# Reordering the first batch of a fused attention and mixer kernel, and the start of its second

## The chip, the cores and the metric

One core of a Trainium2 chip. The metric is the device time of one execution in microseconds (us). The kernel before takes 277.95 us (median of four executions, 277.54 to 278.02). Engines carry their short names in profile lines: PE (TensorE's matmuls), PEld (its weight loads), DVE (VectorE), ACT (ScalarE), POOL (GpSimd), SP (SyncE, which issues transfers).

## The reference

Eight batches of linear attention, then an MLP mixer on its output.

```python
# attention; phi(x) = x + 1 for x > 0, else exp(x)
q_p, k_p = phi(q), phi(k)                          # q, k, v: (8, 8, 576, 64) fp32
kv = einsum('bhsd,bhse->bhde', k_p, v);  z = sum(k_p, axis=2)
x = einsum('bhsd,bhde->bhse', q_p, kv) / (einsum('bhsd,bhd->bhs', q_p, z)[..., None] + 1e-6)
# mixer; x as (8, 576, 512)
h  = maximum(x^T @ w_tok1, 0) @ w_tok2             # over the 576 tokens
u  = x + h^T
out = u + maximum(u @ w_ch1, 0) @ w_ch2            # 512 -> 1536 -> 512
```

## The kernel before

The program gives each engine its instructions in a fixed order, and the traces show them run in it. So a place in that order is a decision: an instruction that waits for data holds up all behind it on its engine. mm1 and mm2 are the two products over tokens, mm3 and mm4 the two over channels. In the names of steps, qtr and qt transpose phi(q), kv forms the product of phi(k) and v, nd forms x's numerator and denominator (num and den divide them), vcast rounds v, warm runs matmuls that compute nothing, and utr transposes u into uT. mm3 and mm4 of one batch are the dense work; a list called `fill` places the next batch's small steps behind numbered pieces of it. While batch 0 is prepared, there is nothing dense to run.

phi, as three instructions per half of k or q (exp on ScalarE, the rest on VectorE):

```python
def phi_exp(nm, n, j0, nj):   nc.scalar.activation(out=e, in_=f, func=AF.Exp)          # f: raw k or q
def phi_add(nm, n, j0, nj):   nc.vector.tensor_scalar(out=y, in0=f, scalar1=1.0, op0=ALU.add)
def phi_end(nm, n, j0, nj):   # e = min(e, 1), then out = max(e, y), both on VectorE
```

mm3 writes a tile in one of four PSUM banks, and a relu empties it (cut):

```python
def mm3(n, mc, kjs=range(NDM)):
    ps = part_of[mc]                              # from the pool ps_big, four banks
    for kj in kjs:
        nc.tensor.matmul(out=ps, lhsT=wc1[:, kj, 128 * mc:128 * mc + 128], rhs=uT[b][:, :, kj], ...)
    if kjs[-1] == NDM - 1:
        nc.scalar.activation(out=cr[b][:, mc, :], in_=ps, func=AF.Relu)
```

mm4 of batch 0 takes its four output tiles from the same four banks, so its first piece needs the relus of mm3's last four tiles. Batch 0's order, and where batch 1's steps stand among its twelve tiles of mm3 (slots 0 to 11) and twelve pieces of mm4 (slots 12 to 23), both cut:

```python
e_first("k", 1); k_first(1, 0); k_first(1, 1)
nd_first(0); warm(24)
e_first("q", 1); q_first(1, 0); vcast(0, 1)
den_first(0); q_first(1, 1); qtr_first(1, [act, act]); kv_first(1, act)
# ... num, mm1 ...
mm2_first(0, [0, 1], False); mm1_first(1, [R])
mm2_first(0, [2, 3], True); mm2_first(1, [0, 1], True)   # True: x added by an identity matmul, ScalarE copies u
mm2_first(1, [2, 3], False)
utr_first(0); mm3 (tiles 0 to 2, half of their products); utr_first(1)

landed[...] = load(nm, 1, c, c_in[0] if nm == "k" and c == 0 else None)     # q right behind k
c2_in += [after(load_wc2(i), landed["q1", 1] if i == 1 else None) for i in range(1, NB)]

fill = [(1, mm2_first_tail)]
fill += [(5, phi k half 0), (8, phi k half 1), (11, phi q half 0), (12, phi q half 1)]
at0 = {"qt0": 13, "qt1": 14, "kv": 15, "nd00": 16, ..., "mm1": 22, "mm2a": 23, ...}
```

`load(..., gate)` issues a transfer only once another has landed: batch 1's k waits for the first quarter of the weight wc1 (issued at 12.86 us in the profile before, 6.9 us to landing; k is issued at 19.73), and wc2's second quarter waits for batch 1's q (issued at 34.95, after 17.83 us of waiting for q).

## Time and profile before

| kernel before | |
|---|---|
| median, range | 277.95 us, 277.54 to 278.02 |
| span of the profiled execution | 275.8 us |
| TensorE busy | 261.5 us, 95% |
| from where TensorE has no gaps | 62 us |

### The profile page before, as it was taken

What the parts mean: (1) busy time and instruction counts of PE and PEld (TensorE: products, weight loads), DVE (VectorE), ACT (ScalarE), POOL (GpSimd) and SP (SyncE); (2) the same over time, 40 slices, a digit from 0 to 9 for tenths busy, and PEclk for the clock granted to TensorE, in tenths of its full rate; (3) what the DMA queues carried; (4) which work ended last, traced back from release to release, by engine and by line L of the source; (5) the groups of instructions that cost most, each with busy time, mean ns of one, the idle gap of its engine ahead of it and who ended that gap; (6) DMA issues with size and microseconds to landing.
All of it is one profiled execution on the core that took longest, in us unless ns stands there. A gap on an engine that the chain in (4) does not pass through costs nothing.

```text
span 275.8 us, 4751 instructions
## 1 busy us (share of the span) xinstructions
PE 261.5 (95%) x1924; PEld 141.0 (51%) x1924; DVE 153.3 (56%) x300; ACT 141.3 (51%) x211; POOL 31.2 (11%) x52
## 2 busy tenths in 40 slices
PE   8678888989999999999999999999999999999993
PEld 8665335544664465445564464445464554444641
DVE  3762274749576957793768347875676271520121
ACT  5634697149974376814666066806673155016400
POOL 4640030004001030011000210011001300000000
PEclk9999999999999999999999999999999999999998
DMA  7999999996002899689918970384045500740043
GB/s 267 293 167 260 358 171 273 400 404 171 2 0 64 205 351 407 272 186 253 402 33 190 351 305 0 71 155 110 0 76 129 133 21 0 134 110 5 2 103 88
DMA packets 45190, 47.73 MB, mean 173 GB/s; under 512 B 25520, under 2 KB 30000, under 8 KB 45168
## 3 DMA queue, kind: packets, MB, share of 16 engines
q1 hardware_dynamic: 37632, 35.53, 41.4%
q0 software_dynamic: 6896, 10.85, 18.2%
q10 hardware_dynamic: 640, 1.05, 1.0%
q8 instruction: 15, 0.25, 0.3%
q14 instruction: 7, 0.06, 0.1%
HBM read 35.85 MB, written 9.44 MB: 164 GB/s over the span
## 4 chain that ended last, share of the span: by engine, by line
PE 87%; ACT 5%; DVE 3%; DMA 2%; issue 1%; SPq 0%; ACTq 0%
PE h_ps L464 32%; PE c_ps L441 28%; PE a_ps L236 5%; PE h_ps L248 5%; PE c_ps L452 4%; PE nd_ps L198 3%; PE kv_ps L157 3%; ACT e L115 2%; DMA q_raw<-in_q_dram 2%; DVE qp L130 1%; PE bank L382 1%; PE tp L168 1%; PE bank L367 1%; PE bank L318 1%; DVE e L129 1%
## 5 line engine op out<-in xcount | busy, mean ns | idle before, releaser
L445 ACT ACTIVATE cr<-c_ps 128x512 bf16<-128x512 f32 x96 | 55.9, 600 | 74.3 <-PE c_ps L441 74.2
L441 PE MATMUL c_ps<-uT,wc 128*128 128x512 bf16 x384 | 91.3, 379 | 1.9 <-ACT uT L407 1.1
L464 PE MATMUL h_ps<-wc,cr 128*128 128x512 bf16 x384 | 88.3, 379 | 0.0
L464 PEld LDWEIGHTS <-cr 128*128 128x128 bf16 x384 | 37.0, 98 | 42.4 <-issue 0.3
L441 PEld LDWEIGHTS <-wc 128*128 128x128 bf16 x384 | 35.8, 98 | 38.6 <-issue 2.7
L481 DVE TENSOR_TENSOR o_sb<-h_ps,u 128x512 f32<-128x512 f32 x32 | 21.7, 688 | 24.1 <-PE h_ps L464 24.0
L486 POOL DMA_DIRECT2D out_dram<-o_sb x24 | 14.9, 625 | 160.7 <-DVE o_sb L481 160.4
L210 DVE TENSOR_TENSOR x<-nd_ps,den 128x512 bf16<-128x512 f32 (+1 forms) x42 | 25.3, 602 | 1.5
L129 DVE TENSOR_SCALAR e<-e 128x1152 bf16<-128x1152 bf16 x30 | 14.5, 485 | 16.3 <-ACT e L115 16.1
L260 DVE TENSOR_TENSOR u<-h_ps,x 128x1024 bf16<-128x1024 f32 x13 | 15.5, 1219 | 13.0 <-PE h_ps L248 13.0
L115 ACT ACTIVATE e<-k_raw 128x1152 bf16<-128x1152 f32 x16 | 18.8, 1172 | 2.6 <-DMA k_raw<-in_k_dram 2.6
L207 DVE TENSOR_SCALAR den<-nd_ps 128x8 f32<-128x8 f32 (+1 forms) x42 | 6.8, 163 | 23.6 <-PE nd_ps L198 23.0
L248 PE MATMUL h_ps<-ar,w2p 128*128 128x512 bf16 x70 | 18.9, 379 | 0.2
L115 ACT ACTIVATE e<-q_raw 128x1152 bf16<-128x1152 f32 x16 | 18.5, 1168 | 0.5 <-DMA q_raw<-in_q_dram 0.5
L141 ACT CAST vs<-v_raw 128x1152 bf16<-128x1152 f32 x14 | 16.3, 1162 | 1.2 <-DMA v_raw<-in_v_dram 1.2
L198 PEld LDWEIGHTS <-qT 128*128 128x128 bf16 x140 | 11.5, 98 | 9.6 <-issue 0.2
L239 ACT ACTIVATE ar<-a_ps 128x512 bf16<-128x512 f32 x14 | 7.6, 595 | 16.9 <-PE a_ps L236 16.9
L198 PE MATMUL nd_ps<-kvbd,qT 128*128 128x130 bf16 x140 | 15.1, 223 | 0.0
L236 PE MATMUL a_ps<-x,w 128*128 128x512 bf16 x56 | 14.4, 379 | 0.0
L491 DVE TENSOR_TENSOR o_sb<-h_ps,ut 128x512 f32<-128x512 f32 x4 | 2.8, 690 | 18.7 <-PE h_ps L464 18.7
L130 DVE TENSOR_TENSOR qp<-e,y 128x1152 bf16<-128x1152 bf16 x16 | 12.1, 759 | 0.6
L121 DVE TENSOR_SCALAR y<-q_raw 128x1152 bf16<-128x1152 f32 x16 | 12.1, 754 | 0.2
(91 smaller groups left out, 222.1 us busy)
## 6 DMA issues: line engine op xcount, KB each, us to landing
k_raw<-in_k_dram SPq DMA_DIRECT2D x16, 576.0 KB, 6.3
q_raw<-in_q_dram SPq DMA_DIRECT2D x16, 576.0 KB, 11.1
v_raw<-in_v_dram SPq DMA_DIRECT2D x16, 576.0 KB, 9.1
out_dram<-o_sb POOLq DMA_DIRECT2D x24, 256.0 KB, 3.9
wc<-in_moe_w_ch_dram POOLq DMA_DIRECT2D x8, 384.0 KB, 8.7
out_dram<-o_sb SPq DMA_DIRECT2D x10, 128.0 KB, 2.3
out_dram<-o_sb ACTq DMA_DIRECT2D x8, 128.0 KB, 2.6
out_dram<-o_sb POOLq DMA_DIRECT2D x6, 128.0 KB, 6.0
```

The costliest lines, as they stand in the source:

```text
L115: nc.scalar.activation(out=e, in_=f, func=AF.Exp)
L129: nc.vector.tensor_scalar(out=e, in0=e, scalar1=1.0, scalar2=None, op0=ALU.min)
L141: copy(out=vs[:, js, :, 0:D], in_=raw["v", n % 2][:, js].rearrange("p j (t d) -> p j t d", t=T))
L198: nc.tensor.matmul(out=o[:, a], lhsT=qT[b][:, t0:t0 + 128], rhs=kvbd[b][:, c, a], start=True, stop=True)
L210: nc.vector.tensor_tensor(out=x[b][:, rs[0]:rs[0] + m, HG * D * g:HG * D * (g + 1)].rearrange("p r (h d) -> p r h d", h=HG), in0=v_[:, :, ...
L236: nc.tensor.matmul(out=ps[:, mt], lhsT=w1t[:, b, ms] if r == R else w1[:, r, ms], rhs=x[b][:, r, :], start=(r == 0), stop=(r == R))
L248: nc.tensor.matmul(out=ps[:, i], lhsT=w2v(kt, r, b), rhs=ar[b][:, kt, :], start=(kt == 0), stop=(kt == NT - 1 and not add))
L260: nc.vector.tensor_tensor(out=u[b][:, rs[0]:rs[0] + m], in0=ps[:, 0:m], in1=x[b][:, rs[0]:rs[0] + m], op=ALU.add)
L441: nc.tensor.matmul(out=ps, lhsT=wc1[:, kj, 128 * mc:128 * mc + 128], rhs=uT[b][:, :, kj], start=(kj == 0), stop=(kj == NDM - 1))
L445: nc.scalar.activation(out=cr[b][:, mc, :], in_=ps, func=AF.Relu)
L464: nc.tensor.matmul(out=ps, lhsT=crt[:, kc, :] if t == 8 else cr[b][:, kc, 128 * r:128 * r + 128], rhs=wc2[:, kc, :], start=(kc == 0), stop ...
L481: nc.vector.tensor_tensor(out=o, in0=ps, in1=u[b][:, r, :], op=ALU.add)
```

## The change

The intent, in three parts. **First batch:** VectorE's work on k's second half moves into a gap; den waits behind q; mm1 of the first half is done in one piece; u's sums all go to VectorE and the four identity matmuls go; the transpositions of u are split. **Batch 1 sooner:** phi of k and q stands from slot 2 instead of slot 5, which puts exp ahead of relus of mm3; three relus go to VectorE; q's load gets a gate; the attention steps from kv on move up one slot (in batch 1's own mixer, which the cut below leaves out, nd moves down one). **End of batch 1's mixer:** mm2 by column halves, and mm3 begun on half of u.

```diff
 e_first("k", 1)
 k_first(1, 0)
+kv_first(0, dve)
 k_first(1, 1)
-nd_first(0)
-warm(24)
 e_first("q", 1)
 q_first(1, 0)
 vcast(0, 1)
-den_first(0)
+nd_first(0)
+warm(14)
 q_first(1, 1)
+den_first(0)
 ...
-mm2_first(0, [0, 1], False)
 mm1_first(1, [R])
-mm2_first(0, [2, 3], True)
-mm2_first(1, [0, 1], True)
-mm2_first(1, [2, 3], False)
-utr_first(0)
-for mc in range(3):
+mm2_first(0, [0, 1])
+mm2_first(0, [2, 3])
+mm2_first(1, [0, 1])
+utr_first([0, 1], act)
+mm2_first(1, [2, 3])
+mm3(0, 0, range(0, 2))
+utr_first([2], act)
+utr_first([3], dve)
+for mc in range(1, 3):
     mm3(0, mc, range(0, 2))
-utr_first(1)
 ...
-load(nm, 1, c, c_in[0] if nm == "k" and c == 0 else None)
+load(nm, 1, c, {"k": c_in[0], "q": c_in[3]}.get(nm) if c == 0 else None)
 ...
+mm3(0, mc, dve=mc in (3, 5, 8))              # relu on VectorE for these
-at0 = {"qt0": 13, "qt1": 14, "kv": 15, "nd00": 16, ...
+at0 = {"qt0": 13, "qt1": 14, "kv": 14, "nd00": 15, ...
-fill = [(1, mm2_first_tail)]
-fill += [(5, phi k 0), (8, phi k 1), (11, phi q 0), (12, phi q 1)]
+fill = [(15, mm2_first_tail)]
+for e_, s_, nm, c in ((2, 3, "k", 0), (4, 5, "k", 1), (7, 8, "q", 0), (9, 10, "q", 1)):
+    fill += [(e_, phi_exp ...), (s_, phi_add ...), (s_, phi_end ...)]
 ...
+fill += [(23, mm4_end 0), (23, mm4_end 1), (23, mm2_half(1, 0)), (23, mm4_end 2),
+         (23, mm2_half(1, 1)), (23, utr(1, [0])), (23, mm2(1, [R])), (23, utr(1, [1])), (23, mm4_end 3)]
+for mc in range(3):
+    mm3(1, mc, range(0, 2))                  # begun on half of u
+utr_tail(0)
```

Each "phi ..." above stands for the lambda of that name; the rest of the diff renames and passes arguments.

More of the change, by code (lines that the diff above doesn't have):

```diff
@@ L176, in qtr_put, with qtr @@
             in_=tp[:, 0:len(ts)].rearrange("p t (a s) -> p t a s", a=2))
-    def qtr(n, c):
+    def qtr(n, c, put=nc.scalar.copy):
         tp = ps_sm.tile([128, 2, 8, 128], BF16, name="tp", tag="sm")
@@ L182, in qtr @@
         for h, ts in enumerate(TS):
-            qtr_put(n, c, ts, tp[:, h], nc.scalar.copy)
+            qtr_put(n, c, ts, tp[:, h], put)
     def qtr_dma(n):
@@ L261, in mm2, with mm2_half @@
                                     in1=x[b][:, rs[0]:rs[0] + m], op=ALU.add)
+    def mm2_half(n, c):
+        b = n % 2
+        cs = COLS[c]
+        for rs in ([0, 1], [2, 3]):
+            ps = ps_sm.tile([128, 2, 512], FP32, name="h_ps", tag="sm")[:, 0].rearrange(
+                "p (r c) -> p r c", r=2)
+            add = rs[0] == 0
+            for i, r in enumerate(rs):
+                if add:
+                    nc.tensor.matmul(out=ps[:, i], lhsT=identity, rhs=x[b][:, r, cs],
+                                     start=True, stop=False)
+                for kt in range(NT):
+                    nc.tensor.matmul(out=ps[:, i], lhsT=w2v(kt, r), rhs=ar[b][:, kt, cs],
+                                     start=(kt == 0 and not add), stop=(kt == NT - 1))
+            if add:
+                nc.scalar.copy(out=u[b][:, 0:2, cs], in_=ps)
+            else:
+                nc.vector.tensor_tensor(out=u[b][:, 2:4, cs], in0=ps, in1=x[b][:, 2:4, cs],
+                                        op=ALU.add)
     def utr(n, js):
@@ L361, in mm1_first @@
         if rs[0] == 0:
-            live["mm1", c] = sm_tile()[:, :, 0:DM // 2]
+            live["mm1", c] = sm_tile()[:, :, 0:DM // 2] if c else bank().rearrange(
+                "p (t c) -> p t c", t=NT)
         ps = live["mm1", c]
@@ L370, in mm1_first, with mm2_first @@
             nc.scalar.activation(out=ar[0][:, :, COLS[c]], in_=ps, func=AF.Relu)
-    def mm2_first(c, rs, add):
+    def mm2_first(c, rs):
         cs = COLS[c]
@@ L376, in mm2_first @@
         for i, r in enumerate(rs):
-            if add:
-                nc.tensor.matmul(out=ps[:, i], lhsT=identity, rhs=x[0][:, r, cs], start=True,
-                                 stop=False)
             for kt in range(NT):
@@ L382, in mm2_first @@
                     nc.tensor.matmul(out=ps[half[e], i], lhsT=w2r[:, kt, :, 2 * r + e],
-                                     rhs=ar[0][:, kt, cs], start=(kt == 0 and not add),
-                                     stop=(kt == NT - 1))
-        dst = u[0][:, rs[0]:rs[0] + 2, cs]
-        if add:
-            nc.scalar.copy(out=dst, in_=ps)
-        else:
-            nc.vector.tensor_tensor(out=dst, in0=ps, in1=x[0][:, rs[0]:rs[0] + 2, cs], op=ALU.add)
+                                     rhs=ar[0][:, kt, cs], start=(kt == 0), stop=(kt == NT - 1))
+        nc.vector.tensor_tensor(out=u[0][:, rs[0]:rs[0] + 2, cs], in0=ps,
+                                in1=x[0][:, rs[0]:rs[0] + 2, cs], op=ALU.add)
     def mm2_first_tail():
-        ps = bank()
+        ps = sm_tile()[:, 0]
         for kt in range(NT):
@@ L397, in mm2_first_tail, with utr_first @@
                                 op=ALU.add)
-    def utr_first(c):
-        tp = bank16().rearrange("p (j r) c -> p j r c", j=2)
-        for i in range(2):
-            j = 2 * c + i
+    def utr_first(js, put):
+        tp = ps_sm.tile([128, 2, 8, 128], BF16, name="tp", tag="sm")[:, 0].rearrange(
+            "p (j r) c -> p j r c", j=2)[:, 0:len(js)]
+        for i, j in enumerate(js):
             for r in range(R):
@@ L405, in utr_first @@
                                     in_=u[0][:, r, 128 * j:128 * j + 128], identity=identity)
-        if c == 0:
-            nc.scalar.copy(out=uT[0][:, :, 0:2].transpose([0, 2, 1, 3]), in_=tp)
-        else:
-            nc.scalar.copy(out=uT[0][:, :, 2], in_=tp[:, 0])
-            nc.vector.tensor_copy(out=uT[0][:, :, 3], in_=tp[:, 1])
+        put(out=uT[0][:, :, js[0]:js[-1] + 1].transpose([0, 2, 1, 3]), in_=tp)
     def w2_put(kt):
@@ L433, with mm3 @@
     part_of = {}
-    def mm3(n, mc, kjs=range(NDM)):
+    def mm3(n, mc, kjs=range(NDM), dve=False):
         b = n % 2
@@ L443, in mm3 @@
                              start=(kj == 0), stop=(kj == NDM - 1))
-        if kjs[-1] == NDM - 1:
+        if kjs[-1] == NDM - 1 and dve:
+            nc.vector.tensor_scalar(out=cr[b][:, mc, :], in0=ps, scalar1=0.0, scalar2=None,
+                                    op0=ALU.max)
+        elif kjs[-1] == NDM - 1:
             nc.scalar.activation(out=cr[b][:, mc, :], in_=ps, func=AF.Relu)
@@ L552 @@
     k_first(0, 0)
-    warm(80)
+    warm(76)
     k_first(0, 1)
@@ L559 @@
     qtr_first(0, [dve, dve])
-    kv_first(0, dve)
     e_first("k", 1)
     k_first(1, 0)
+    kv_first(0, dve)
     k_first(1, 1)
-    nd_first(0)
-    warm(24)
     e_first("q", 1)
@@ L569 @@
     vcast(0, 1)
+    nd_first(0)
+    warm(14)
+    q_first(1, 1)
     den_first(0)
-    q_first(1, 1)
     qtr_first(1, [act, act])
@@ L575 @@
     num_first(0, R, 1)
-    mm1_first(0, range(R))
     nd_first(1)
+    mm1_first(0, range(R1))
     den_first(1)
     num_first(1, 0, 2)
+    mm1_first(1, [0, 1])
     num_first(1, 2, 2)
+    mm1_first(1, [2, 3])
     num_first(1, R, 1)
-    mm1_first(0, [R])
-    mm1_first(1, [0, 1])
-    mm1_first(1, [2, 3])
-    mm2_first(0, [0, 1], False)
     mm1_first(1, [R])
-    mm2_first(0, [2, 3], True)
-    mm2_first(1, [0, 1], True)
-    mm2_first(1, [2, 3], False)
-    utr_first(0)
-    for mc in range(3):
+    mm2_first(0, [0, 1])
[7 more added lines that the diff above has]
+    for mc in range(1, 3):
         mm3(0, mc, range(0, 2))
-    utr_first(1)
     for nm in "kqv":
         for c in range(2):
-            landed[nm + "1", c] = load(nm, 1, c, c_in[0] if nm == "k" and c == 0 else None)
+            landed[nm + "1", c] = load(nm, 1, c, {"k": c_in[0], "q": c_in[3]}.get(nm) if c == 0 else None)
     c2_in += [after(load_wc2(i), landed["q1", 1] if i == 1 else None) for i in range(1, NB)]
@@ L607, in steps @@
         if n < 4:
-            out_ += [(f"qt{g}", lambda g=g: qtr(n, g)) for g in range(2)]
+            puts = [nc.scalar.copy, nc.vector.tensor_copy if n == 1 else nc.scalar.copy]
+            out_ += [(f"qt{c}", lambda c=c: qtr(n, c, puts[c])) for c in range(2)]
         for i, rs in enumerate(([0, 1], [2, 3], [4])):
@@ L611, in steps @@
                 out_.append((f"nd{i}{g}", lambda g=g, rs=rs: nd(n, g, rs)))
-        out_ += [("mm1", lambda: mm1(n)), ("mm2a", lambda: mm2(n, [0, 1])),
-                 ("mm2b", lambda: mm2(n, [2, 3], n == 1)), ("mm2t", lambda: mm2(n, [R]))]
-        if n < 2:
-            out_.append(("ut", lambda: utr(n, [0, 1])))
-            if n % 2:
-                out_.append(("utt", lambda: utr_tail(n // 2)))
-        else:
+        out_.append(("mm1", lambda: mm1(n)))
+        if n > 1:
+            out_ += [("mm2a", lambda: mm2(n, [0, 1])), ("mm2b", lambda: mm2(n, [2, 3])),
+                     ("mm2t", lambda: mm2(n, [R]))]
             out_ += [("uta", lambda: utr_dma(n, [0, 1])), ("utb", lambda: utr_dma(n, [2, 3]))]
@@ L641, in m4_0 @@
             mm4(0, t, [kc], wait=True)
-    big = [lambda mc=mc: mm3(0, mc, range(2, 4)) for mc in range(3)] + m3(0, 3) + \
+    big = [lambda mc=mc: mm3(0, mc, range(2, 4)) for mc in range(3)] + \
+        [lambda mc=mc: mm3(0, mc, dve=mc in (3, 5, 8)) for mc in range(3, NCH)] + \
         [lambda kc=kc: m4_0(kc) for kc in range(NCH)]
-    at0 = {"qt0": 13, "qt1": 14, "kv": 15, "nd00": 16, "nd01": 17, "nd10": 18,
-           "nd11": 19, "nd20": 20, "nd21": 21, "mm1": 22, "mm2a": 23, "mm2b": 23, "mm2t": 23,
-           "ut": 23, "utt": 23}
@@ L648 @@
-    fill = [(1, mm2_first_tail)]
-    fill += [(5, lambda: phi("k", 1, 0)), (8, lambda: phi("k", 1, 1)),
-             (11, lambda: phi("q", 1, 0)), (12, lambda: phi("q", 1, 1))]
-    fill += [(13, lambda: vcast(1, 0)), (14, lambda: vcast(1, 1, nc.vector.tensor_copy))]
-    fill += [(18 + kt, lambda kt=kt: w2_put(kt)) for kt in range(NT)]
-    fill += [(at0[nm], fn) for nm, fn in steps(1) if nm[:2] in ("kv", "qt", "nd", "mm")]
-    fill += [(23, lambda: mm4_end(0, 0))]
-    fill += [(at0[nm], fn) for nm, fn in steps(1) if nm[:2] == "ut"]
@@ L656 @@
-    fill += [(23, lambda t=t: mm4_end(0, t)) for t in range(1, R)]
+    at0 = {"qt0": 13, "qt1": 14, "kv": 14, "nd00": 15, "nd01": 16, "nd10": 17,
+           "nd11": 18, "nd20": 19, "nd21": 20, "mm1": 21}
+    fill = [(15, mm2_first_tail)]
+    for e_, s_, nm, c in ((2, 3, "k", 0), (4, 5, "k", 1), (7, 8, "q", 0), (9, 10, "q", 1)):
+        fill += [(e_, lambda nm=nm, c=c: phi_exp(nm, 1, 2 * c, 2)),
+                 (e_ if c == 0 and nm == "k" else s_, lambda nm=nm, c=c: phi_add(nm, 1, 2 * c, 2)),
+                 (s_, lambda nm=nm, c=c: phi_end(nm, 1, 2 * c, 2))]
@@ new lines @@
+    fill += [(12, lambda: vcast(1, 0)), (12, lambda: vcast(1, 1, nc.vector.tensor_copy))]
+    fill += [(16 + kt, lambda kt=kt: w2_put(kt)) for kt in range(NT)]
+    fill += [(at0[nm], fn) for nm, fn in steps(1)]
+    fill += [(23, lambda: mm4_end(0, 0)), (23, lambda: mm4_end(0, 1)),
+             (23, lambda: mm2_half(1, 0)), (23, lambda: mm4_end(0, 2)),
+             (23, lambda: mm2_half(1, 1)), (23, lambda: utr(1, [0])),
+             (23, lambda: mm2(1, [R])), (23, lambda: utr(1, [1])), (23, lambda: mm4_end(0, 3))]
@@ L657 @@
     run(big, sorted(fill, key=lambda e: e[0]))
+    for mc in range(3):
+        mm3(1, mc, range(0, 2))
+    utr_tail(0)
     load_all(3, "kvq")
-    big = m3(1) + m3t + m4(0, [4, 5, 6, 7, 8])
-    at1 = {"kv": 8, "qt0": 11, "qt1": 12, "nd00": 13, "nd01": 14, "nd10": 15,
-           "nd11": 16, "nd20": 17, "nd21": 18, "mm1": 20, "mm2a": 21, "mm2b": 22, "mm2t": 24,
+    big = [lambda mc=mc: mm3(1, mc, range(2, 4)) for mc in range(3)] + m3(1, 3) + m3t + m4(0, [4, 5, 6, 7, 8])
+    at1 = {"kv": 8, "qt0": 11, "qt1": 12, "nd00": 14, "nd01": 15, "nd10": 16,
+           "nd11": 17, "nd20": 18, "nd21": 19, "mm1": 20, "mm2a": 21, "mm2b": 22, "mm2t": 24,
```

## The prediction

> **What bounds the kernel now.** I read the page first: busy time by engine, then the forty slices.
>
> ```profile
> PE 261.5 (95%) x1924; PEld 141.0 (51%) x1924; DVE 153.3 (56%) x300; ACT 141.3 (51%) x211; POOL 31.2 (11%) x52
> ...
> PE   8678888989999999999999999999999999999993
> ...
> DMA  7999999996002899689918970384045500740043
> ```
>
> TensorE is the bound, but its gaps all lie in the first nine slices (62 us) and at the very end. From 62 us to about 270 us it has no gap, so the change can only win by bringing TensorE to that dense part sooner; whatever is won by 62 us is kept, and nothing later can be won. DMA is also full in the first 62 us. Next, the timeline of the first 64 us, for where TensorE waits:
>
> ```profile
> 8.42 0.68 PE L168 MATMUL bank<-identity,qp 128*128 128x128 bf16 x9 [0.98 <-DVE qp L130]
> ...
> 14.74 0.68 PE L168 MATMUL bank<-identity,qp 128*128 128x128 bf16 x9 [1.46 <-DVE qp L130]
> ...
> 25.97 1.46 PE L441 MATMUL c_ps<-uT,wc 128*128 128x512 bf16 x6 [1.10 <-ACT uT L407]
> ...
> 28.54 1.27 PE L441 MATMUL c_ps<-uT,wc 128*128 128x512 bf16 x4 [0.67 <-ACT uT L409]
> ...
> 38.59 2.09 PE L464 MATMUL h_ps<-wc,cr 128*128 128x512 bf16 x8
> ...
> 41.78 0.68 PE L168 MATMUL tp<-identity,qp 128*128 128x128 bf16 x9 [1.10 <-DVE qp L130]
> ...
> 60.32 1.05 PE L271 MATMUL tp<-identity,u 128*128 128x128 bf16 x16 [0.49 <-ACT u L258]
> ...
> 62.25 7.93 PE L441 MATMUL c_ps<-uT,wc 128*128 128x512 bf16 x36
> ```
>
> Four marks are to be seen: the second q transposition at 14.74, the first uT at 25.97 (dense mm3 from 28.54), mm4 of batch 0 from 38.59, dense mm3 of batch 1 at 62.25. Last, what the transfers do, from the timeline of GpSimd and the issues in single narrow windows:
>
> ```profile
> 34.95 2.24 POOL L535 DMA_DIRECT2D wc<-in_moe_w_ch_dram x3 [17.83 <-DMA q_raw<-in_q_dram]
> ```
>
> Batch 1's k is issued at 19.73 and lands 7.2 and 9.5 us after its two issues (27.0 and 29.7 us), its q after 11.6 and 12.4 (32.2 and about 34.5), its v about 36 and 37.4. The last quarter of wc1 is issued at 15.1 and lands after 14.1 us, at 29.2. The next wc2 pieces wait for q to land, are issued from 34.95 and land after 5.9, 7.1 and 8.2 us: 40.8, 42.9, 44.7.
>
> [...] 576 KB of k takes 3.7 us to land when alone at the start, 7.2 to 9.5 beside the weights. [...] the chain has 60 mm4 matmuls in 12.95 us, 216 ns. [...] the nearest row of the trace, the 128x512 add from PSUM, takes 688, ScalarE's relu 600. So three relus moved to VectorE are no faster, only elsewhere. [...] the 1152-element min at 13.15, while GpSimd issues wc1, took 740 ns, against 460 for its kind elsewhere.
>
> **The change, part by part.** I carry TensorE's clock through the new order with durations of the timeline (max 0.76, min 0.46, q add 0.76, ScalarE exp 1.16, relu 0.6, cast 1.16; 512-column matmul 0.216, 256-column 0.108; mm2's eight of batch 0 0.67).
>
> First batch, to 16 us. In the new order VectorE fills its gap at 9.80 with k's relu (to 10.56), then kvbd (11.16, 0.27 later than now), k's min (11.62), and q's add, min and max without den in between: 12.38, 12.84, 13.60. The second transposition starts at 13.65 instead of 14.74: 1.1 us won. kv follows to 15.5, kvbd on ScalarE to 16.15, nd to 17.2 (now 18.38).
>
> To 25 us. num runs on VectorE 17.25 to 18.87. mm1 of half 0 is now complete in one piece, 10 x 0.108 to 18.3; its relu ends at 19.05. mm1 of half 1 follows num and ends at 19.4. Four mm2 groups end at 20.1, 20.8, 21.45 and, after the first transposition, 22.85. The four identity matmuls are gone (4 x 0.108 = 0.43 us of TensorE), and u's sums sit on VectorE: 20.85, 21.57, 22.25, 23.6. The first transposition waits for the second sum, 21.6 to 22.2; ScalarE's copy of uT (1.01) ends 23.27; mm3 starts 23.35 instead of 25.97. The last transpositions and copies end 24.8, under mm3. Dense mm3 from 25.2, against 28.9 now (28.54 plus the wait for uT's last quarter): **3.7 us won so far**.
>
> Batch 0's mm3, from 25.2. Left are 6 + 36 matmuls, 42 x 0.216 = 9.07: to 34.3, where before it was 38.59 with the tail's 0.64, which is moved. But phi is pulled forward in ScalarE's and VectorE's fixed order, ahead of relus that TensorE's four PSUM banks need, and its data do not come sooner. exp of k's two halves: the first finds its data (27.4), the second waits to 29.7; enough banks are free. exp of q's second half stands ahead of the relus of mm3's last two tiles. q is now issued after wc1's last quarter (29.2 instead of 20.65), [...] the bytes ahead of q are the same, so I put its landing unchanged, near 34.9. Then exp to 36.05, two relus to 36.55 and 37.1. mm4 does its first two tiles to 34.7 and must wait for those banks to about 37.2: **2.3 to 2.5 us of new waiting**. Mm4's first piece ends 37.4; by TensorE's work it stands where it now stands at 39.45, less the tail.
>
> From there q is ready, so the waits of 1.10 and 0.42 us for qp at 41.78 and 43.73 are gone: qt0 and qt1 (0.5 each), kv (1.14) and two pieces of mm4 (0.86 each) end at 41.3. mm4's fourth piece needs wc2's second quarter at 40.8: just met. Then the tail 0.43, six nd slots of 0.86 + 0.24 or 0.12 at VectorE's pace (now 1.1 us per slot), mm1 10 x 0.216 = 2.16, two mm4 pieces: 52.9.
>
> End of batch 1's mixer. mm2 by halves has the same columns (20 x 0.108 = 2.16). ScalarE takes half of u in 0.58 us, VectorE the other in 0.69 behind the output sums (0.69 each). I find waits of 0.35, 0.2, 0.2 and 0.5 us for PSUM and u, where now there are 0.49, 0.65 and smaller. mm3's first six half tiles (1.3 us) fill the time in which uT's second half is copied. So mm3's second halves begin at about 59.5, with 1.3 us of mm3 done: comparable to 58.2 against 62.25, **4.0 us won**.
>
> Batch 1's mm3: ScalarE is full there now (9.96 of 10 us in 70 to 80), and its chain shifts by about 3.2 us only, since its first relu comes later relative to the work done. nd is moved one slot later to fit; I charge 0.3 us. Sum: 4.0 - 0.3 = 3.7, and 277.98 - 3.7 = 274.3. I round to 274.2.
>
> **Rivals.** (a) The whole early gain is kept and the qp waits vanish too: 3.7 + 1.5 + about 0.7 = 5.9 us, 272.1. For it: TensorE is the bound everywhere later. Against it: q lands at 34.5, and wc2's second quarter, gated by q, lands 5.9 us after that; TensorE cannot pass mm4's fourth piece before 40.8, whatever the first batch wins. It needs q a microsecond sooner, which the cleaner order of transfers could give. (b) The new gate costs: [...] k's first packets came some 3.5 us after its issue at 19.73 (the bandwidth by microsecond shows queue 1 starting near 23.2), at a lighter load 0.8 us after (42.94). If q starts at 32.5, it lands near 36.3, both the relus and wc2 slip by 1.4, and the time is 275.7. (c) ScalarE or VectorE becomes the bound in batch 1's mm3 and gives back 1 to 2 us: 275.5. For: the 9.96. Against: three relus go to VectorE in the earlier phase, and nd's slot is moved. (d) The early microseconds vanish wholly, 278: it would take all of (b) and (c).
>
> **Range and chances.** The centre is my sum. It has about 1.5 us of uncertainty from q's landing, 1 us from small waits that I could not see, and up to 1 us from ScalarE in batch 1, which mostly add in squares: 272.5 to 276.0. Faster by over 2% needs below 272.5 (277.98 / 1.02), that is rival (a) nearly whole: 0.12. Within 2%: 0.87. Slower needs over 5.5 us of new waits: 0.01.
>
> **What would show it.** In the new trace: second q transposition near 13.7; mm3's first matmul near 23.4; q's issue near 29 and its landing near 35; mm4's first piece split by a wait of over 2 us released by relus of mm3, with ScalarE waiting for q before it; no wait for qp at batch 1's transpositions; mm3's half tiles of batch 1 near 58; the rest of the trace shifted whole by 3 to 4 us. Wrong if q lands before 33.5 (then near 272) or after 36 (near 276), or if TensorE shows new gaps between 60 and 80 us.

The sum: 4.0 - 0.3 = 3.7 us, and 277.98 - 3.7 = 274.3, rounded to 274.2, stands on durations of the timeline. That q lands at an unchanged time, near 34.9, because the same bytes lie ahead of it, was the estimate. k at the start, with its 3.7 us, was not quite alone: q was issued 0.5 us behind it (1.26 after 0.74).

## More of the kernel before

The next lines are the stretches view of the kernel before: the stretch, its length, then busy time (and number of instructions) of PE, PEld, DVE, ACT and POOL, the granted TensorE clock, the transfers' share and GB/s.

```profile
0.00:24.00 24.00, 18.82 (x288) 16.42 (x290) 13.10 (x28) 12.06 (x16) 10.85 (x19) 1.00 0.99 238
24.00:34.00 10.00, 8.14 (x51) 3.98 (x49) 2.46 (x4) 5.33 (x9) 0.00 (x0) 1.00 1.11 335
34.00:42.00 8.00, 6.86 (x35) 2.96 (x33) 5.85 (x9) 8.00 (x12) 2.24 (x3) 1.00 0.96 189
42.00:62.00 20.00, 18.36 (x152) 9.83 (x150) 11.10 (x26) 9.11 (x13) 0.00 (x0) 1.00 1.03 364
```

TensorE has gaps in all four stretches (some of its busy time in the first is the matmuls of warm, which compute nothing), and the transfers' share is near 1 in all of them (0.96 to 1.11).

In 34 to 42 us ScalarE is busy throughout (8.00 of 8 us).

## The result, and the profile after

The kernel after takes 273.67 us (273.19 to 273.82, four executions), against 277.95. The ratio is 0.9846 (95% interval 0.9829 to 0.9863). A ratio here is the mean time of one kernel's fast runs over the mean of the other's of the same rounds, so it is not quite the ratio of the medians. That is 4.3 us by the medians, 3.7 us by the two profiled spans (275.8 and 272.1), and within 2%, as predicted. A later repetition on another occasion gave 273.21 and a ratio of 0.9833.

The page of the kernel after, the two lines that answer to the first ones of the prediction:

```profile
PE 258.1 (95%) x1897; PEld 140.9 (52%) x1916; DVE 156.6 (58%) x308; ACT 137.3 (50%) x205; POOL 30.2 (11%) x52
...
PE   8589979989999999999999999999999999999993
```

The same four stretches as before:

```profile
0.00:24.00 24.00, 18.25 (x289) 16.38 (x290) 14.94 (x31) 12.34 (x15) 10.19 (x19) 1.00 1.02 242
24.00:34.00 10.00, 10.00 (x51) 4.60 (x49) 6.89 (x12) 7.24 (x11) 0.00 (x0) 1.00 1.07 312
34.00:42.00 8.00, 6.26 (x69) 3.45 (x69) 4.70 (x8) 6.35 (x10) 2.30 (x3) 1.00 0.98 209
42.00:62.00 20.00, 18.91 (x124) 10.60 (x125) 12.03 (x29) 6.86 (x11) 2.44 (x4) 1.00 1.01 354
```

From 24 to 34 us TensorE is now full. In 34 to 42 us it waits more than before (6.26 busy instead of 6.86): the work of these stretches is not the same, since everything is now some four microseconds sooner. The timeline of TensorE after, at the marks of the prediction:

```profile
13.89 0.68 PE L168 MATMUL bank<-identity,qp 128*128 128x128 bf16 x9 [0.61 <-DVE qp L130]
...
23.21 0.59 PE L450 MATMUL c_ps<-uT,wc 128*128 128x512 bf16 x2 [0.43 <-ACT uT L419]
...
24.09 10.09 PE L450 MATMUL c_ps<-uT,wc 128*128 128x512 bf16 x46
34.02 0.73 PE L476 MATMUL h_ps<-wc,cr 128*128 128x512 bf16 x2
35.95 1.73 PE L476 MATMUL h_ps<-wc,cr 128*128 128x512 bf16 x5 [1.21 <-ACT cr L457]
37.51 0.67 PE L168 MATMUL tp<-identity,qp 128*128 128x128 bf16 x9
...
41.10 1.02 PE L476 MATMUL h_ps<-wc,cr 128*128 128x512 bf16 x3 [0.31 <-DMA wc<-in_moe_w_ch_dram]
...
59.60 4.70 PE L450 MATMUL c_ps<-uT,wc 128*128 128x512 bf16 x21
```

ScalarE in the same stretch (L115 is exp, L457 relu):

```profile
32.67 1.16 ACT L115 ACTIVATE e<-q_raw 128x1152 bf16<-128x1152 f32 x1 [1.13 <-DMA q_raw<-in_q_dram]
33.74 0.58 ACT L457 ACTIVATE cr<-c_ps 128x512 bf16<-128x512 f32 x1
34.25 1.16 ACT L115 ACTIVATE e<-q_raw 128x1152 bf16<-128x1152 f32 x1
35.32 1.06 ACT L457 ACTIVATE cr<-c_ps 128x512 bf16<-128x512 f32 x2
```

The second transposition of q comes 0.85 us sooner (14.74 before), the first mm3 2.8 us (25.97), mm4 4.6 us (38.59; 4.0 without the 0.6 us of mm2's tail, which has moved behind it). Then two matmuls of mm4 run and the third starts only at 35.95: the new wait, and relus end it. ScalarE shows what held them: exp of q's first half waits 1.13 us for q, and the last two relus stand behind exp of the second half. The transposition at 37.51 no longer waits for qp. mm4's fourth piece at 41.10 waits for wc2.

The chain of waits that ended last, of the kernel after, in this stretch (start, length, what):

```profile
14.96 13.23 DMA wc<-in_moe_w_ch_dram
...
28.62 5.55 DMA q_raw<-in_q_dram
...
34.71 6.35 DMA wc<-in_moe_w_ch_dram
...
41.10 0.38 PE h_ps L476
```

Here the chain leaves the engines altogether: wc1's last quarter, behind it q, behind that wc2's second quarter, each issued when the one ahead has landed. In this execution all the work that the first batch saved ends at a transfer of wc2, by 0.31 us. In the repetition mm4's fourth piece starts at 40.68 without a wait (wc2 had taken 4.8 us from issue to landing, not 6.35), and the chain runs from q's first half through exp and the relus on ScalarE into mm4. So two limits lie within half a microsecond of each other: q with the order on ScalarE, and wc2 behind q.

### The profile page after: what moved, and what is told of

It is laid out like the page before. It is cut to its first block, busy times and chain, and to the rows that moved or that the text cites. A ratio compares the mean times of both kernels' runs of the same rounds, so it can differ in the third digit from the quotient of the medians.

```text
span 272.1 us, 4720 instructions
## 1 busy us (share of the span) xinstructions
PE 258.1 (95%) x1897; PEld 140.9 (52%) x1916; DVE 156.6 (58%) x308; ACT 137.3 (50%) x205; POOL 30.2 (11%) x52
## 3 DMA queue, kind: packets, MB, share of 16 engines
q10 hardware_dynamic: 640, 1.05, 1.1%
## 4 chain that ended last, share of the span: by engine, by line
PE 82%; DMA 12%; POOL 2%; ACT 1%; issue 1%; SPq 1%; DVE 0%; ACTq 0%; POOLq 0%
PE h_ps L476 33%; PE c_ps L450 27%; DMA wc<-in_moe_w_ch_dram 7%; PE a_ps L236 5%; PE h_ps L248 5%; PE c_ps L464 4%; PE nd_ps L198 3%; DMA k_raw<-in_k_dram 3%; PE kv_ps L157 3%; DMA q_raw<-in_q_dram 2%; POOL wc L542 1%; PE tp L168 1%; SPq L107 1%; POOL w L553 1%; PE tp L291 0%
## 5 line engine op out<-in xcount | busy, mean ns | idle before, releaser
L457 ACT ACTIVATE cr<-c_ps 128x512 bf16<-128x512 f32 x93 | 54.1, 600 | 72.7 <-PE c_ps L450 72.6
L115 ACT ACTIVATE e<-k_raw 128x1152 bf16<-128x1152 f32 x16 | 18.8, 1175 | 3.1 <-DMA k_raw<-in_k_dram 3.1
L115 ACT ACTIVATE e<-q_raw 128x1152 bf16<-128x1152 f32 x16 | 18.6, 1170 | 1.7 <-DMA q_raw<-in_q_dram 1.7
L260 DVE TENSOR_TENSOR u<-h_ps,x 128x1024 bf16<-128x1024 f32 x12 | 14.3, 1218 | 8.1 <-PE h_ps L248 8.1
L248 PE MATMUL h_ps<-ar,w2p 128*128 128x512 bf16 x60 | 16.2, 379 | 0.1
```

The source lines that it names most:

```text
L248: nc.tensor.matmul(out=ps[:, i], lhsT=w2v(kt, r, b), rhs=ar[b][:, kt, :], start=(kt == 0), stop=(kt == NT - 1 and not add))
L260: nc.vector.tensor_tensor(out=u[b][:, rs[0]:rs[0] + m], in0=ps[:, 0:m], in1=x[b][:, rs[0]:rs[0] + m], op=ALU.add)
```

## The experiments

All are correct unless said otherwise. Three groups ran on different occasions; times are compared through the runs of the kernel before beside them (277.90, 277.74 and 277.95).

**First batch alone.** The kernel before, with the new first batch and nothing else.

```diff
 # order of the first batch, mm1_first, mm2_first, utr_first: as after
 # loads, fill, mm2 and mm3 of batch 1, mm2's tail: as before
```

> Only the first batch is new; the later slots, the gate of q and the whole mm2 of batch 1 are as before. Theory (the first batch wins about 4 us; the later parts win about as much as the wait for q and for wc2's second quarter takes back): dense mm3 about 4 us sooner than before, exp of q still behind all but the last relu of mm3, so no wait for q; 274.0 us (273.6 to 274.5), i.e. within 0.5 us of the whole change. Rival (the first batch's win runs into the data and is lost, and the gain is the later parts'): 276 us or more.

Measured: 274.27 us (273.71 to 274.93), ratio 0.9870. TensorE's timeline:

```profile
35.68 1.90 PE L453 MATMUL h_ps<-wc,cr 128*128 128x512 bf16 x7 [0.42 <-DMA wc<-in_moe_w_ch_dram]
...
38.29 0.68 PE L168 MATMUL tp<-identity,qp 128*128 128x128 bf16 x9 [0.70 <-DVE qp L130]
...
58.98 5.34 PE L430 MATMUL c_ps<-uT,wc 128*128 128x512 bf16 x24
```

In time as the theory had it. mm4 waits for wc2's first quarter (0.42 us), which the theory did not name, and for no relu, and the old waits for qp are still there (1.1 us in all, 1.5 before). The first batch alone brings 3.6 of the 4.3 us.

**The rest alone.** The converse: the kernel after, with the old first batch.

```diff
 # order of the first batch, mm1_first, mm2_first, utr_first: as before
 # all else as after
```

> Only the later parts are new, on the old first batch. Theory (the parts share one limit, the transfers): mm3 then ends near 38 us, q has landed by then, no wait of relus on q, and the waits for qp are gone; the later parts are worth about 2.3 us here though they are worth under 0.5 us behind the new first batch: 275.6 us (275.0 to 276.3). The two parts' gains then sum to about 6.2 us, while together they give 4.3. Rival (gains add up, as the stretches of the trace suggest: 3.9 for the first batch, 0.3 for the rest): 277.4 to 277.8 us.

Measured: 276.14 us (275.55 to 276.40), ratio 0.9934.

```profile
28.78 9.47 PE L461 MATMUL c_ps<-uT,wc 128*128 128x512 bf16 x42 [0.67 <-ACT uT L429]
38.08 2.39 PE L487 MATMUL h_ps<-wc,cr 128*128 128x512 bf16 x7
...
61.92 2.32 PE L461 MATMUL c_ps<-uT,wc 128*128 128x512 bf16 x10
```

mm4 starts at 38.08 and waits little (TensorE is idle 0.23 us in all from 38 to 40 us): four microseconds later, q has landed. So the later parts are worth 1.8 us by themselves, in the range that the theory gave, and far from the rival's 0.1 to 0.5. The two gains sum to 1.96% and together they are 1.54% (1.67% in the repetition). Taken together, the intervals leave about 0.25% of doubt on that difference of 0.3 to 0.4%, so by time alone the overlap is barely told from noise. The traces support it: the wait of 1.2 us for relus at mm4 stands in the whole change and in neither half.

**A delay of 1 us.** 19 matmuls on the identity ahead of mm3's fourth tile, into that tile's own bank (1.22 us busy in the trace).

```diff
     ps = part_of[mc]
+    if n == 0 and mc == 3:
+        for _ in range(19):
+            nc.tensor.matmul(out=ps[:, 0:128], lhsT=identity, rhs=identity, start=True, stop=True)
```

> The whole change, and 19 more 128-column matmuls on the identity (about 1.0 us of TensorE) just before mm3's fourth tile of batch 0, into that tile's own bank, which its first matmul then overwrites. Theory (between 34 and 41 us TensorE waits for relus held up by q, then for wc2): at most 0.3 us slower than the whole change, 273.7 to 274.0. Rival (TensorE's own work is the bound in the first 62 us): 1.0 us slower, 274.7.

Measured: 274.36 us (273.47 to 274.97), ratio 0.9873. The profiled execution took 273.74:

```profile
35.81 1.73 PE L479 MATMUL h_ps<-wc,cr 128*128 128x512 bf16 x5 [0.32 <-ACT cr L460]
...
59.50 4.70 PE L453 MATMUL c_ps<-uT,wc 128*128 128x512 bf16 x21
```

In this execution the delay is swallowed whole: the wait for relus shrinks from 1.21 to 0.32 us and the last mark is at 59.50, as in the change itself. But the five executions fall in two lots, 273.5 to 273.7 and 274.4 to 275.0, and the median lies between theory (274.0 at most) and rival (274.7). Against the repetition of the change (273.21) the median is 1.2 us slower, which is the rival's figure. Why some executions pay and others not stays open; the others were not traced, so this run alone decides nothing.

**A delay of 3 us.** The same with 56 matmuls (3.29 us busy in the trace).

> The same with 56 matmuls, about 3.0 us. Theory: the slack of about 1.8 us (the wait at 34.5 to 36, and the wait for wc2 behind it) is used up and the rest shows: 1.2 us slower than the whole change (0.7 to 1.8), 274.9. Rival (TensorE's own work is the bound): 3.0 us slower, 276.7.

Measured: 274.82 us, ratio 0.9906. One of six executions, the profiled one, took 277.37; the other five lie at 274.72 to 275.35. In the profiled one q and wc2 came late (q was issued at 29.49 us instead of 28.20, because wc1's last quarter landed late, and wc2 at 36.69 instead of 34.71):

```profile
43.37 1.02 PE L479 MATMUL h_ps<-wc,cr 128*128 128x512 bf16 x3 [0.59 <-DMA wc<-in_moe_w_ch_dram]
```

3 us of extra work cost 1.2 us by the medians (274.82 less 273.67), 1.6 us against the repetition; both lie in the theory's 0.7 to 1.8 and far from the rival's 3. So TensorE has well over a microsecond of slack in this stretch; its work is not the bound there.

**q and v without their transfers** (wrong result). phi and cast of batch 1 read a tile filled at the start; the transfers still run.

```diff
+fake = cr[1].rearrange("p c s -> p (c s)")[:, 0:4 * TD].bitcast(FP32)...   # filled with 0.25 at the start
-f = raw[nm, n % 2][:, j0:j0 + nj]...
+f = given(nm, n, j0, nj)...       # fake for q and v of batch 1
```

> The whole change with a wrong result on purpose: batch 1's exp, add and cast of q and v read a tile that is filled at the start, so they wait for no transfer; the transfers themselves still run, and wc2's second quarter still waits for q to land. Theory (two gates in a row, q's and then wc2's): the wait of 1.2 us for relus shrinks to about 0.5 us, the wait for wc2 grows by as much, mm4's fourth piece still starts near 41 us; 273.5 to 273.9, no gain over the whole change. Rival (the wait for q is what holds the time): 272.3.

Measured: 275.42 us (272.76 to 275.70), ratio 0.9895: slower, which neither expected. The trace does show the mechanism of the theory:

```profile
34.55 1.73 PE L481 MATMUL h_ps<-wc,cr 128*128 128x512 bf16 x5 [0.50 <-ACT cr L462]
...
41.31 1.02 PE L481 MATMUL h_ps<-wc,cr 128*128 128x512 bf16 x3 [1.91 <-DMA wc<-in_moe_w_ch_dram]
```

The wait for relus fell from 1.21 to 0.50 us, the one for wc2 rose from 0.31 to 1.91, and mm4's fourth piece starts at 41.31 instead of 41.10: no gain, as expected. The trace is not as clean as that sounds: in this execution q was issued at 29.57 us (28.20 in the change), because wc1's last quarter landed late, and wc2 at 36.02 (34.71), so the 1.91 us are the gates and this lateness together. The loss in time comes after it. The stretches view by single microseconds, with the granted clock third from the end:

```profile
40.00:41.00 1.00, 0.00 (x0) 0.00 (x0) 0.26 (x1) 1.00 (x2) 0.00 (x0) 1.00 1.22 198
...
43.00:44.00 1.00, 1.00 (x7) 0.70 (x7) 0.83 (x3) 0.00 (x0) 0.00 (x0) 0.50 1.22 204
...
46.00:47.00 1.00, 1.00 (x9) 0.63 (x8) 0.90 (x3) 0.00 (x0) 0.00 (x0) 0.94 1.01 387
```

Shortly after the gap of 1.91 us the clock was halved, for about 3.4 us (the clock's shortfall summed over 42 to 47 us is 1.7 us, as much as the excess of this span, 273.8, over 272.1). That the gap brought it is not shown. Two of the four executions show a clock of 0.994, the fastest 1.000; one of 275.24 us shows 1.000 too and stays unexplained. (The mean of 0.997 of the kernels before and after is no slow stretch: there the granted clock falls below 1, to 0.50, only in the last 2 us, when TensorE has finished.)

**The same, and wc2 issued without its gate.**

```diff
-c2_in += [after(load_wc2(i), landed["q1", 1] if i == 1 else None) for i in range(1, NB)]
+c2_in += [load_wc2(i) for i in range(1, NB)]
```

> The same, and wc2's other three quarters are issued right behind the first, not behind q. Theory: mm4's fourth piece starts near 39.6 instead of 41.1 us; 1.5 us faster than the whole change, 272.2 (271.8 to 272.7). Rival (the order of ScalarE and VectorE holds this stretch, not the transfers): 273.4 to 273.8.

Measured: 273.00 us (271.99 to 273.44), ratio 0.9821, between the two. mm4's fourth piece starts at 40.40, sooner than 41.10 but not at 39.6, and the reason is on ScalarE:

```profile
30.45 1.16 ACT L120 ACTIVATE e<-k_raw 128x1152 bf16<-128x1152 f32 x1 [1.22 <-DMA k_raw<-in_k_dram]
```

k landed about a microsecond later than in the last experiment (there this exp starts at 29.29) and held up the same relus. Whether wc2's earlier issue delayed k is not shown by one execution: k landed as late with all gates in place in the run with the relus on ScalarE (exp at 30.62).

**Without the new gate of q.**

```diff
-load(nm, 1, c, {"k": c_in[0], "q": c_in[3]}.get(nm) if c == 0 else None)
+load(nm, 1, c, c_in[0] if nm == "k" and c == 0 else None)
```

> The whole change without its new gate: batch 1's q is issued right after its k, as before, not behind the last quarter of wc1. Theory (the same bytes lie ahead of q either way): q lands within 0.7 us of now, 34.2 us; 273.4 to 274.4. Rival (the gate is what brings q in time): q lands over 1 us later and the time is 275 us.

Measured: 273.47 us, ratio 0.9868, three executions at 272.94 to 273.91 and one at 276.39 with a clock of 0.991. wc2's second quarter, which waits for q, is issued at 35.29 us instead of 34.71. That does not show that the gate brings q sooner: with the gate, the same issue lies between 34.30 and 36.69 us in the other profiled runs that keep the condition on all of q. Two smaller things can be seen. In the two profiled runs without the gate and with the new first batch, this one and the first batch alone, mm4's first piece waits for wc2's first quarter (0.61 and 0.42 us); in none with the gate does it. And the gate passes a late wc1 on to q: in three slower profiled executions (3 us of delay, q and v free, relus on ScalarE) q is issued at 29.49 to 30.12 us, in the others with the gate at 27.96 to 28.50. No effect of the gate on the time can be told.

**The three relus back on ScalarE.**

```diff
-mm3(0, mc, dve=mc in (3, 5, 8))
+mm3(0, mc, dve=False)
```

> The whole change with mm3's three relus back on ScalarE. Theory: ScalarE has 1.5 us more to do before mm4, of which 1.8 us of its waits for k and q take most; the relus of the last two tiles come up to 0.5 us later, and that is hidden by the wait for wc2; 273.6 to 274.0. Rival (ScalarE is the bound there): 1.0 to 1.5 us slower, 275.

Measured: 274.21 us, 272.71 to 276.76, ratio 0.9882 (0.9826 to 0.9938). Inconclusive: the spread covers both. The profiled execution (276.76) waited 2.5 us for relus in all instead of 1.2, no single wait over 1.2 us, with the halved clock again (0.61 and 0.50 in 38 to 41 us), and q was issued late, at 30.12 us.

**Two of u's sums back on ScalarE**, with the identity matmuls, beside a repetition of the whole change.

```diff
-    mm2_first(0, [2, 3])
-    mm2_first(1, [0, 1])
+    mm2_first(0, [2, 3], True)        # identity matmul adds x, ScalarE copies u
+    mm2_first(1, [0, 1], True)
```

> The whole change itself once more, on the chip and in the rounds of the next three, to compare with and to see how far its executions spread: 273.7 us (273.2 to 274.5); [...] an execution near 275.5 with a clock below 0.995 may be among them.

> The whole change with two of u's four sums of batch 0 as before: x added by an identity matmul (4 x 0.108 = 0.43 us of TensorE) and copied out by ScalarE. Theory: mm3 starts 0.3 to 0.5 us later, and the wait for q's relus at 34.5 to 36 us swallows it; at most 0.2 us slower than the whole change. Rival (TensorE's work counts there): 0.4 us slower.

Measured: the change 273.21 us (273.02 to 273.39), ratio 0.9833, with no slow execution among the four; the sums back 273.39 us, ratio 0.9848. TensorE of the run with the sums back:

```profile
34.92 2.39 PE L483 MATMUL h_ps<-wc,cr 128*128 128x512 bf16 x8
...
42.04 0.41 PE L198 MATMUL nd_ps<-kvbd,qT 128*128 128x130 bf16 x4
```

and of the change, repeated:

```profile
36.00 1.73 PE L476 MATMUL h_ps<-wc,cr 128*128 128x512 bf16 x6 [1.24 <-ACT cr L457]
...
42.27 0.41 PE L198 MATMUL nd_ps<-kvbd,qT 128*128 128x130 bf16 x4
```

The first mm3 came 1.4 us later (24.12 against 22.75), more than I expected, and mm4 then ran without waiting and was done no later: nd starts at 42.04 against 42.27. A part of the change that truly saves 1.4 us in the first batch is worth about 0.2 us by the medians (0.4 by the ratios, with one execution at 274.53). The trace shows why: with the sums back, wc2's second quarter lands at 40.4, and mm4's fourth piece starts at 40.45, against 40.68 in the repetition. q's landing helped: wc2, which waits for q, was issued at 34.30 there and at 34.76 in the repetition.

**mm2's tail into the wait.**

```diff
-fill = [(15, mm2_first_tail)]
+fill = [(11, mm2_first_tail)]
```

> The whole change with mm2's tail of batch 0 (two matmuls, 0.43 to 0.64 us) moved from behind mm4's fourth piece to just before mm4. Theory (TensorE waits there for relus and then for wc2, so this work is free there and costs its full time where it is now): mm4's fourth piece still near 41.1 us, nd right behind it, 0.5 us faster than the whole change (0.3 to 0.7), 273.2. Rival (TensorE's work is the bound, order does not matter): no difference.

Measured: 273.22 us, ratio 0.9833: no difference from the change, a miss. In the profiled execution nd did come 0.4 us sooner (41.90), though q's second half landed some 0.35 us later there and moved the relus along. By time it is nothing.

**The tail, the relus ahead of exp, and wc2 sooner.**

```diff
-fill = [(15, mm2_first_tail)]
-... (7, 8, "q", 0), (9, 10, "q", 1)
+fill = [(11, mm2_first_tail)]
+... (7, 8, "q", 0), (11, 11, "q", 1)
-after(load_wc2(i), landed["q1", 1] if i == 1 else None)
+after(load_wc2(i), landed["q1", 0] if i == 1 else None)
```

> The same, and exp of q's second half behind the relus of mm3's last tiles, and wc2's second quarter issued when q's first half has landed, not its second. Theory (both gates loosened): mm4's first piece no longer waits over 0.5 us, the fourth piece starts at 40 to 40.8 us; 0.9 to 1.3 us faster than the whole change, 272.5. Rival (v then lands later and kv waits instead): as the run with the tail alone, 273.2 or slower.

Measured: 271.67 us (271.32 to 272.13), ratio 0.9783 (0.9767 to 0.9798). This beats both kernels: 1.5 us faster than the change, and 2.2% faster than before.

```profile
34.46 2.11 PE L476 MATMUL h_ps<-wc,cr 128*128 128x512 bf16 x8
...
39.53 1.03 PE L476 MATMUL h_ps<-wc,cr 128*128 128x512 bf16 x4
...
57.28 6.79 PE L450 MATMUL c_ps<-uT,wc 128*128 128x512 bf16 x30
```

mm4's first two pieces run through, the fourth starts at 39.53 without a wait, and the last mark stands at 57.28 instead of 59.17 in the repetition of the change. How much of the 1.5 us is the order on ScalarE and how much is wc2's earlier issue (33.12 instead of 34.76) was not run apart; the tail alone was nothing. The traces suggest that both were needed: with the tail alone wc2 had landed by 40.6 us, and mm4's fourth piece, held by the relus, came only at 41.03; here wc2 landed at 39.3, just ahead of 39.53, so with the later issue the fourth piece would likely have waited for it.

## Why the prediction was right

The time (274.2 predicted, 273.67 measured) and its steps held.

- **First batch.** Second transposition 13.65 predicted, 13.89 measured; first mm3 23.35 and 23.21. Dense mm3 was put at 25.2 with 42 matmuls left; measured are 46 in one run from 24.09, so the 42 last start near 24.95. mm4 34.3 and 34.02. The first batch alone measured 3.6 us against the 3.7 of the text.
- **New wait at mm4.** The mechanism was right: relus, behind exp of q on ScalarE, behind q's landing. Its size was the term most off: 2.3 to 2.5 us predicted, about 1.5 us measured (the third tile at 35.95 after the second ended near 34.45). q landed near 34.2 and not 34.9, so exp of its second half, the one that the text had waiting, did not wait for it; the wait for q (1.13 us) came at exp of the first half, which the text did not charge. The last tile followed the third at once.
- **wc2 behind it.** "Just met" was right to 0.3 us: the fourth piece starts at 41.10. In the repetition it starts at 40.68 with no wait for wc2. Gate after gate is shown by the chain of waits, and the run without q's and v's transfers agrees: there the wait moved to wc2, in an execution in which q was late as well.
- **End of batch 1's mixer.** mm3's second halves at 59.5 predicted, 59.60 measured; the small waits, three and not four, come to 1.05 us where the text had 1.25.
- **Batch 1's mm3.** 0.3 us was charged. 3.95 us at the last mark (62.25 less 59.60, plus 1.3 us of mm3 already done) become 3.7 us in the span, so 0.25.
- **Rivals.** (a), the whole gain, did not come, for the reason given; the last experiment loosens those gates and reaches 271.67, where (a) had put 272.1. (b), that the gate of q costs 1.4 us, did not come: q landed near 34.2 and not 36.3. Whether the gate helps or costs a little stays open. (c) is small.

Where I did not see far enough: the prediction treats transfers as fixed times. They vary from execution to execution: behind the same gates, wc2's second quarter was issued between 34.30 and 36.69 us and took 4.8 to 6.6 us from issue to landing. And in two profiled executions TensorE's clock stood at half for about 3.4 us. Both made single experiments unclear.

On the durations that the prediction took from the trace: the matmul pace is confirmed by the chain of the kernel after (48 matmuls of mm3 in 10.36 us, 216 ns). VectorE's relu of 128x512 from PSUM took 683 ns (the add beside it in the prediction 688), ScalarE's 597 at the median. A min of 1152 elements beside GpSimd's issue of wc2 took 580 ns instead of 460; no run isolates the cause.

## What to carry to other kernels

When work is made faster ahead of a chain of transfers, ask when each transfer lands and what it gates, before counting the gain: here 1.4 us of true saving was worth 0.2 to 0.4. On an engine that runs in order, put an instruction that may wait for a transfer behind those that release buffers for the bound engine (here 1.5 us, together with an earlier issue of wc2). Two changes that each win alone can share one limit, so measure them alone and together.
